# Two feature blocks of a gated feed-forward product by seven half-block products

## The chip, the cores and the metric

The kernel runs on one core of a Trainium2 chip. The metric is the device time of one execution in microseconds (us); smaller is better. The core's engines, as the profile names them: PE is TensorE (matmuls; PEld its weight loads), DVE is VectorE, ACT is ScalarE, POOL is GpSimd, SP is SyncE, which here only issues DMAs. All engines run their own instructions in program order and wait for each other by semaphores. SBUF is the memory that all engines work in, PSUM the one that TensorE writes its results to; PSUM is used here in eight banks of 512 f32 values for each of 128 partitions.

## The reference

Attention with projected keys and values (8 batches, 8 heads, 1024 positions, head size 64, 64 projected keys), whose output is the input of a gated feed-forward layer (8192 tokens, model width 512, hidden width 1536):

```python
k_proj = einsum('ks,bhsd->bhkd', E, k)
v_proj = einsum('ks,bhsd->bhkd', F, v)
scores = (q @ k_proj^T) / sqrt(64)
x = softmax(scores) @ v_proj            # then heads side by side: 8192 x 512
g = x @ w_gate
silu = g / (1 + exp(-g))
val = x @ w_val
out = (silu * val) @ w_out
```

The inputs are f32; the kernel loads them as bf16 and multiplies in bf16 with f32 sums.

## The kernel before

The 8192 tokens are worked in 16 chunks of 512 (c = 0 to 15), two for each batch: chunk 2b and chunk 2b + 1. For each chunk, `xT` holds the attention output transposed: 128 partitions x 4 blocks of the model width x 512 tokens. The hidden width is worked in 12 blocks of 128 features (f = 0 to 11). The main loop at the end of the program runs over all (c, f), with counter t = 12c + f; each turn has two slots, 2t and 2t + 1, into which the next batch's attention work is put by hand.

One turn:

- `f_g(c, f)`: the gate product, four matmuls of 512 tokens into a bank `gps` (pool "g", two banks), then ScalarE's SiLU into an f32 tile `th` (line 541). In some blocks, listed in `TANGENT`, a tanh and two VectorE operations (lines 538, 553, 556) take its place; blocks 10 and 11 of chunks 2 to 14 are not among them.
- slot 2t
- `f_v(c, f)`: the value product, four matmuls of 512 into a bank `vps` (pool "v", two banks in turn), then VectorE multiplies `th` by it into `hT[c][:, f]` (line 550)
- what `late[t]` holds: the output product of the chunk before, and sums for it
- slot 2t + 1

The output product (`f_m`, lines 676 to 686) already goes by seven products of half blocks (Strassen). For each of two token halves p it makes products m = 3, 4, 5, 2, 1, 6, 7, each of six matmuls of 256 columns (line 634), at blocks 0, 1, 2, 3, 4, 4, 5 for p = 0 and 6, 7, 8, 9, 10, 10, 11 for p = 1 of the chunk that follows. Products 3, 4, 5, 2 share a bank "y", and 1, 6, 7 a bank "z". Between them come `m_34` (ScalarE copy, GpSimd sum L653), `m_52` (ScalarE copy L658), `m_16` (VectorE L663, GpSimd L664) and `m_7` (VectorE L669, and the output DMA on SP's queue). The sums of hidden blocks that these products need are `h_sum` (line 617): m = 5 and 2 on GpSimd, one feature pair (f, f + 6) at a time as soon as block f + 6 is done (blocks 6 to 11); m = 1, 6, 7 on VectorE, whole, in blocks 1 to 3 of the next chunk.

Attention for the next batch in the slots: `u_KV` (projections, L176, evacuated by ScalarE L184 and VectorE L189), `u_S` (scores L367 and exponential L375), `u_R` (row sum L397 and reciprocal L398 on VectorE), `u_N` (division L412 and a running check L428 on GpSimd), `u_AD` and `u_TD` (transposes by DMA on SP's queue), and `u_PVt` (L471), which makes `xT` with four ScalarE copies (L480) out of the banks "a", "a", "y", "z". `u_PVt` stands in block 10 of chunk 2 and of the odd chunks 3 to 13, and in block 4 of the even chunks 4 to 14. `u_R` for the next batch falls into blocks 7 and 9 of the even chunks 4 to 12, and into blocks 8 and 10 of chunk 2.

Loads of q, k and v for the next batch are issued from GpSimd's queue. q has a pool of four buffers, `s1` one of three.

Of the kernel before, what the change touches and what calls it, by code (L numbers as in the profile page):

```python
# [9 lines left out]
AF = mybir.ActivationFunctionType  # L10
ALU = mybir.AluOpType
AX = mybir.AxisListType
BF16 = mybir.dt.bfloat16
FP32 = mybir.dt.float32

B = 8
H = 8
S = 1024
D = 64
# [3 lines left out]
P = 128  # L23
# [3 lines left out]
NFT = DFF // P  # L27
CH = 2
CW = 512
NIT = B * CH * NFT  # L30
NC = B * CH
HF = NFT // 2
HC = DM // 2
HT = CW // 2
ENG = [getattr(mybir.EngineType, n) for n in ("PE", "DVE", "Activation", "SP", "Pool")]
TANGENT = [(c, f) for c in range(CH) for f in range(NFT)] + [
    x for b in range(2, B) for x in ((2 * b - 2, 8 if b == 2 else 7), (2 * b - 1, 1))
]
BY_DMA = [(b, ch) for b in range(1, B) for ch in range(CH)]


@with_exitstack
def kernel(
# [19 lines left out]
    nc = tc.nc  # L63
# [2 lines left out]
    const = ctx.enter_context(tc.tile_pool(name="const", bufs=1))  # L66
    w_pool = ctx.enter_context(tc.tile_pool(name="weights", bufs=1))
    kv_pool = ctx.enter_context(tc.tile_pool(name="kv", bufs=1))
    q_pool = ctx.enter_context(tc.tile_pool(name="qbf", bufs=4))
    aw = ctx.enter_context(tc.tile_pool(name="aw", bufs=2))  # L70
    x_pool = ctx.enter_context(tc.tile_pool(name="xT", bufs=1))
    h_pool = ctx.enter_context(tc.tile_pool(name="hT", bufs=2))
    fw = ctx.enter_context(tc.tile_pool(name="fw", bufs=3))
# [22 lines left out]
    wv = w_pool.tile([P, NKT, DFF], BF16, name="wv")  # L96
# [3 lines left out]
    kb, vb, qb, xT, hT = {}, {}, {}, {}, {}  # L100
# [3 lines left out]
    def batch(t, b):  # L104
        return t[bass.ds(turn_of[0], 1)].rearrange("o h s d -> (o h) s d") if turn_of else t[b]

    def load_k(b, h0=0, h1=H):
        if b or maxed:
            kb[b] = kv_pool.tile([P, H, NJ, D], BF16, name="kb", tag="kb")
        nc.gpsimd.dma_start(  # L110
            out=kb[b][:, h0:h1].rearrange("p h j d -> p h (j d)"),
            in_=batch(k, b)[h0:h1].rearrange("h (p j) d -> p h (j d)", j=NJ),
        )
# [10 lines left out]

    def load_q(b, ch, js=(0, 4), hs=(0, H)):
        if js[0] == 0 and hs[0] == 0:
            qb[b, ch] = q_pool.tile([P, H, 4, D], BF16, name="qb", tag="qb")
        js, hs = slice(*js), slice(*hs)
        nc.gpsimd.dma_start(  # L129
            out=qb[b, ch][:, hs, js, :].rearrange("p h j d -> p h (j d)"),  # L130
            in_=batch(q, b)[hs].rearrange("h (p c j) d -> p c h j d", c=2, j=4)[:, ch, :, js, :].rearrange(
                "p h j d -> p h (j d)"
            ),
        )
# [16 lines left out]
    maxed = []  # L151
# [4 lines left out]
    def bank(where, shape, dt, name):  # L156
        if where == "a" and ring["wide"]:
            where = "aaz"[ring["n"] % 3]
            ring["n"] += 1
        pool, tag = banks[where]  # L160
        return pool.tile(shape, dt, name=name, tag=tag)
# [150 lines left out]
    qT, ee, rr, AA, AT = {}, {}, {}, {}, {}  # L312
    by_dma = list(BY_DMA)

# [195 lines left out]
    gp = {}  # L510
# [3 lines left out]
    def f_mm(c, f, w, i=None):  # L514

        if i != 1:


            where = "y" if (c, f, w) == (0, 2, 0) else "gv"[w]
            half[c, f, w] = bank(where, [P, CW], FP32, where + "ps")  # L520
        ps = half[c, f, w]
        x = xT[divmod(c, CH)]
        ts = slice(0, CW) if i is None else slice(256 * i, 256 * (i + 1))
        for kt in range(NKT):
            nc.tensor.matmul(  # L525
                out=ps[:, ts],
                lhsT=(wg, wv)[w][:, kt, f * P : (f + 1) * P],
                rhs=x[:, kt, ts],
                start=(kt == 0),
                stop=(kt == NKT - 1),  # L530
            )
        return ps

    def f_g(c, f, i=None):
        ps = f_mm(c, f, 0, i)
        th = fw.tile([P, CW], FP32, name="th", tag="th")
        if (c, f) in TANGENT and not maxed:
            nc.scalar.activation(out=th[:], in_=ps[:], func=AF.Tanh, scale=0.5)  # L538
            gp[0] = (ps, th)
        else:  # L540
            nc.scalar.activation(out=th[:], in_=ps[:], func=AF.Silu)  # L541
            gp[0] = (None, th)

    def f_v(c, f, i=None):
        ps = f_mm(c, f, 1, i)
        g, th = gp.pop(0)
        if f == 0:
            hT[c] = h_pool.tile([P, NFT, CW], BF16, name="hT", tag="hT")
        if g is None:
            nc.vector.tensor_tensor(out=hT[c][:, f, :], in0=th[:], in1=ps[:], op=ALU.mult)  # L550
            return
        s1 = fw.tile([P, CW], FP32, name="s1", tag="s1")
        nc.vector.scalar_tensor_tensor(
            out=s1[:], in0=th[:], scalar=1.0, in1=g[:], op0=ALU.add, op1=ALU.mult
        )
        nc.vector.scalar_tensor_tensor(
            out=hT[c][:, f, :], in0=s1[:], scalar=0.5, in1=ps[:], op0=ALU.mult, op1=ALU.mult
        )
# [226 lines left out]
    def general():  # L785
# [6 lines left out]
        with tc.For_i(0, B) as turn, tc.manual_schedule():  # L792
            turn_of.append(turn)
            b = 0
            load_k(b)
            load_v(b)
            u_KV(b)
            u_KT(b)
            for ch in range(CH):
                c = CH * b + ch  # L800
                load_q(b, ch)
                for u in range(4 * ch, 4 * ch + 4):
                    u_T(b, u)
                    u_S(b, u)
                    u_R(b, u)
                    u_N(b, u)
                    u_A(b, u)
                u_PVt(b, ch, (0, 1), ("aa", "yz"))
                for f in range(NFT):
                    f_g(c, f)  # L810
                    f_v(c, f)
                for m in (1, 2, 5, 6, 7):
                    h_sum(c, m, 0, HF, nc.vector)
                for n in range(14):
                    f_m(c, n)

    with tc.manual_schedule():
# [3 lines left out]
        for i in range(2):  # L821
            nc.scalar.dma_start(
                out=kraw[i][:],
                in_=k[0, 2 * i : 2 * i + 2].rearrange("h (p j) d -> p h (j d)", j=NJ),
# [4 lines left out]
        ]  # L829
        nc.sync.dma_start(out=ef[0][:], in_=E)  # L830
        load_q(0, 0, (0, 2))
        load_k(0, 4, 8)
        zeros = fw.tile([P, CW], BF16, name="zeros", tag="s1")
        nc.vector.memset(zeros[:], 0.0)
        make_identity(nc, ident_fp[:])
        make_identity(nc, ident_bf[:])
# [24 lines left out]

        dve, act = nc.vector, nc.scalar
        load_q(0, 0, (2, 4))
        nc.gpsimd.dma_start(out=ef[1][:], in_=F)
        load_v(0, (0, 4, 6, 8))
# [5 lines left out]
        for h in range(4):  # L871
            for n in range(2):
                eng = act if (h, n) == (3, 1) else dve
# [90 lines left out]
        late = defaultdict(list)  # L964
# [4 lines left out]
        for c in range(1, NC):  # L969
            for f in range(HF):  # L970
                for m in (5, 2):
                    late[c * NFT + HF + f].append((h_sum, c, m, f, f + 1))
            if c == NC - 1:
                late[c * NFT + HF].append((h_sum, c, 6, 0, HF, nc.vector))
                for f in (0, 2, 4):
                    for m in (1, 7):
                        late[c * NFT + HF + f + 1].append((h_sum, c, m, f, f + 2, nc.vector))
            else:
                for i, m in enumerate((1, 6, 7)):
                    late[(c + 1) * NFT + 1 + i].append((h_sum, c, m, 0, HF, nc.vector))  # L980
                for n, f in enumerate((0, 1, 2, 3, 4, 4, 5, 6, 7, 8, 9, 10, 10, 11)):
                    late[(c + 1) * NFT + f].append((f_m, c, n))

        for s, fn in ((38, u_sum), (40, u_flag), (88, u_bad)):
            put(48 * (B - 2) + s, fn)
        for t in range(NIT):
            c, f = divmod(t, NFT)
            ring["wide"] = c < 2
            i = 1 if t < 2 else None
            f_g(c, f, i)  # L990
            run_slot(2 * t)
            f_v(c, f, i)
            for fn, *a in late.pop(t, ()):
                fn(*a)
            run_slot(2 * t + 1)
# [34 lines left out]
```

## Time and profile before

| what | us |
|---|---|
| median of 3 runs (548.88 to 549.53) | 549.27 |
| the profiled execution: its time | 548.71 |
| the profiled execution: span from first to last instruction | 547.2 |
| TensorE matmuls busy | 534.7 |
| VectorE busy | 317.3 |
| GpSimd busy | 303.7 |
| ScalarE busy | 262.2 |
| one 512-wide operation on VectorE, L550: mean | 0.684 |
| one 256-wide operation on VectorE, L663: mean | 0.422 |
| h_sum on GpSimd, 128x256 bf16: mean (shortest 0.657, longest 1.321) | 0.686 |
| h_sum on VectorE, 128x1536 bf16: mean (most often 0.95, longest 1.462) | 1.089 |

The granted TensorE clock of the core is 0.998 of full speed. A chunk in the steady part takes some 32.5 us, a block 2.38 us, or 3.0 us where two output products stand in it.

How to read it: busy time is the union of an engine's instructions. A matmul's row gives its latency (0.273 us for 256 columns), while the next one starts 0.109 us after it; so the pitch is read from the start times of rows that follow each other, not from the mean. In a timeline, equal instructions of one engine are merged ("x4") and the second number is from the first start to the last end. "[0.62 <-PE yps L634]" means that the engine was idle for 0.62 us before, until that instruction ended.

### The profile page before, as it was taken

The numbers are of one execution on the slowest core, as the hardware profiler recorded it, in microseconds if no ns is written. First come the engines' busy times: TensorE is split into PE (matmuls) and PEld (weight loads), VectorE is DVE, ScalarE is ACT, GpSimd is POOL, SyncE is SP. The second block draws the span as 40 slices with busy tenths as digits, with TensorE's granted clock in tenths as the row PEclk, the third lists the DMA queues.
The fourth block names the chain that finished last, engine by engine and source line by source line (L and its number), as shares of the span: only waits on it lengthen the run. The fifth ranks groups of instructions, "written<-read, shape, count | busy, mean of one in ns | idle before, by whom it ended". The sixth has DMA issues, their size and how long they took to land.

```text
span 547.2 us, 9325 instructions
## 1 busy us (share of the span) xinstructions
PE 534.7 (98%) x3496; PEld 314.1 (57%) x3558; DVE 317.3 (58%) x546; ACT 262.2 (48%) x441; POOL 303.7 (56%) x428
## 2 busy tenths in 40 slices
PE   8999999999999999999999999999999999999996
PEld 4654545555556655556555565566555665555665
DVE  3787895557347654667456483465735765343553
ACT  3564454574446634556435554455444663443331
POOL 6962494487616864096632966258661666416172
PEclk9999999999999999999999999999999999999999
DMA  9999969929931797109930199114990123011003
GB/s 201 192 196 191 167 145 185 178 77 147 205 73 40 145 208 149 40 2 200 208 94 38 56 185 218 45 40 94 206 201 2 39 78 78 38 40 40 13 27 120
DMA packets 112226, 62.92 MB, mean 115 GB/s; under 512 B 65968, under 2 KB 103856, under 8 KB 112176
## 3 DMA queue, kind: packets, MB, share of 16 engines
q0 software_dynamic: 43952, 29.49, 37.6%
q1 hardware_dynamic: 67392, 31.46, 24.3%
q10 hardware_dynamic: 832, 1.31, 0.8%
q8 instruction: 29, 0.48, 0.3%
q14 instruction: 21, 0.17, 0.1%
HBM read 60.29 MB, written 16.78 MB: 141 GB/s over the span
## 4 chain that ended last, share of the span: by engine, by line
PE 94%; DMA 2%; POOL 1%; issue 1%; ACT 0%; DVE 0%; POOLq 0%; DVEq 0%; ACTq 0%
PE vps L525 30%; PE gps L525 29%; PE yps L634 25%; PE sc L367 3%; DMA wv<-in_moe_w_val_dram 2%; PE kvp L176 2%; PE yps L568 2%; PE pv L471 1%; POOL vb L120 0%; POOL qb L129 0%; POOL AA L412 0%; PE kvp L215 0%; PE kvp L200 0%; PE qTp L332 0%; PE pv L451 0%
## 5 line engine op out<-in xcount | busy, mean ns | idle before, releaser
L525 PE MATMUL vps<-xT,wv 128*128 128x512 bf16 (+1 forms) x755 | 195.4, 377 | 2.0 <-DMA wv<-in_moe_w_val_dram 0.9
L525 PE MATMUL gps<-xT,wg 128*128 128x512 bf16 (+1 forms) x733 | 193.0, 377 | 1.7
L550 DVE TENSOR_TENSOR hT<-th,vps 128x512 bf16<-128x512 f32 x156 | 106.7, 684 | 146.7 <-PE vps L525 121.5
L541 ACT ACTIVATE th<-gps 128x512 f32<-128x512 f32 x156 | 93.2, 597 | 176.1 <-PE gps L525 156.0
L617 POOL TENSOR_TENSOR hs<-hT 128x256 bf16<-128x256 bf16 x180 | 118.6, 686 | 40.6 <-DVE hT L550 40.0
L525 PEld LDWEIGHTS <-wv 128*128 128x128 bf16 x776 | 74.1, 98 | 91.0 <-issue 6.5
L634 PEld LDWEIGHTS <-hs 128*128 128x128 bf16 x900 | 88.1, 98 | 34.6 <-issue 0.6
L525 PEld LDWEIGHTS <-wg 128*128 128x128 bf16 x776 | 74.1, 98 | 51.4 <-issue 0.2
L664 POOL TENSOR_TENSOR tt<-tt,ysb 128x512 f32<-128x512 f32 x28 | 35.5, 1269 | 101.5 <-DVE tt L663 101.5
L412 POOL TENSOR_TENSOR AAd<-ee,zr 128x512 bf16<-128x512 f32 x56 | 58.4, 1043 | 41.6 <-ACT ee L375 17.6
L634 PE MATMUL yps<-ws,hs 128*128 128x256 bf16 x540 | 68.6, 273 | 0.2 <-DVE ysb L703 0.2
L397 DVE TENSOR_REDUCE zr<-ee 128x8 f32<-128x512 f32 x64 | 43.4, 678 | 20.4 <-ACT ee L375 20.4
L617 DVE TENSOR_TENSOR hs<-hT 128x1536 bf16<-128x1536 bf16 (+1 forms) x49 | 50.0, 1026 | 0.1
L634 PE MATMUL yps<-ws,hT 128*128 128x256 bf16 x360 | 48.8, 273 | 0.3
L634 PE MATMUL yps<-wo,hs 128*128 128x256 bf16 x360 | 48.6, 273 | 0.1
L653 POOL TENSOR_TENSOR tt<-xs 128x256 f32<-128x256 f32 x30 | 22.9, 763 | 39.7 <-ACT xs L651 39.7
L634 PEld LDWEIGHTS <-hT 128*128 128x128 bf16 x360 | 35.2, 98 | 16.0
L375 ACT ACTIVATE ee<-sc 128x512 f32<-128x512 f32 x64 | 35.7, 606 | 4.3 <-PE sc L367 2.9
L658 ACT COPY ysb<-yps 128x512 f32<-128x512 f32 x30 | 17.6, 586 | 27.3 <-PE yps L634 27.3
L651 ACT COPY xs<-yps 128x512 f32<-128x512 f32 x30 | 17.7, 590 | 25.1 <-PE yps L634 25.0
L538 ACT ACTIVATE th<-gps 128x512 f32<-128x512 f32 x35 | 20.9, 598 | 16.5 <-PE gps L525 16.5
L480 ACT CAST xT<-pv 128x512 bf16<-128x512 f32 x56 | 28.8, 599 | 0.0
(112 smaller groups left out, 403.7 us busy)
## 6 DMA issues: line engine op xcount, KB each, us to landing
out_dram<-ysb SPq DMA_DIRECT2D x27, 512.0 KB, 3.0
qb<-in_q_dram POOLq DMA_DIRECT2D x14, 512.0 KB, 15.2
kb<-in_k_dram POOLq DMA_DIRECT2D x7, 1024.0 KB, 10.0
vb<-in_v_dram POOLq DMA_DIRECT2D x7, 1024.0 KB, 14.8
wo<-in_moe_w_out_dram POOLq DMA_DIRECT2D x2, 768.0 KB, 21.6
out_dram<-ysb SPq DMA_DIRECT2D x6, 256.0 KB, 2.4
kraw<-in_k_dram ACTq DMA_DIRECT2D x2, 512.0 KB, 4.7
qb<-in_q_dram POOLq DMA_DIRECT2D x4, 256.0 KB, 7.9
```

The source lines that it names most:

```text
L375: nc.scalar.activation(out=e[:].rearrange("p h j k -> p (h j k)"), in_=ps[:].rearrange("p a k -> p (a k)"), func=AF.Exp, scale=scale,)
L397: nc.vector.reduce_sum(out=z, in_=e[:], axis=AX.X)
L412: eng.tensor_tensor(out=a.rearrange("p j h k -> p h j k"), in0=ee.pop((b, u))[:], in1=r.unsqueeze(3).to_broadcast([P, 4, 2, KP]), op=ALU.mult,
L480: nc.scalar.copy(out=xT[b, ch][:, kt, :], in_=ps[:])
L525: nc.tensor.matmul(out=ps[:, ts], lhsT=(wg, wv)[w][:, kt, f * P : (f + 1) * P], rhs=x[:, kt, ts], start=(kt == 0), stop=(kt == NKT - 1),)
L538: nc.scalar.activation(out=th[:], in_=ps[:], func=AF.Tanh, scale=0.5)
L541: nc.scalar.activation(out=th[:], in_=ps[:], func=AF.Silu)
L550: nc.vector.tensor_tensor(out=hT[c][:, f, :], in0=th[:], in1=ps[:], op=ALU.mult)
L617: eng.tensor_tensor(out=hs[c, m][:, fs, :], in0=quarter(hT[c], *a)[:, fs], in1=quarter(hT[c], *b)[:, fs], op=op,)
L634: nc.tensor.matmul(out=ps, lhsT=lhsT, rhs=ws[m][:, f, :] if rhs is None else rhs, start=(start and f == 0), stop=(f == HF - 1), skip_group ...
L653: nc.gpsimd.tensor_tensor(out=t[:, 0], in0=xs[:, 0], in1=xs[:, 1], op=ALU.add)
L664: nc.gpsimd.tensor_tensor(out=t[:], in0=t[:], in1=yo[c, p][:, 1:3], op=ALU.subtract)
```

## The change

In chunks 2 to 14 the value products of blocks 10 and 11 are made together. They are a product of a 256 x 512 weight by a 512 x 512 input; both are cut into two by two halves (weights: 128 features x 256 model; input: 256 model x 256 tokens), and the four result quarters come from seven products of halves in place of eight, each of two matmuls of 256 tokens. The sums of weight halves are made once, in chunk 2, on VectorE (`p_w`); the sums of input halves for every chunk (`p_x`), on GpSimd in even chunks (blocks 2, 3, 3, 5) and on VectorE in odd ones (blocks 6 to 9). SiLU of blocks 10 and 11 goes into one tile `thp`. The value product of block 10 makes products 3, 4 and 1, that of block 11 products 5, 2, 6 and 7, with seven VectorE operations that put the quarters together and multiply.

For the space, q's pool goes from four to two buffers and the two of batch 0 get tags of their own, whose space the sums use later; `s1` goes from three buffers to one. The `h_sum` of m = 5 and 2 for the last two feature pairs moves from blocks 10 and 11 behind block 0 of the next chunk.

```diff
+PAIR = (10, 11)
+PAIRED = range(2, NC - 1)
...
-    q_pool = ctx.enter_context(tc.tile_pool(name="qbf", bufs=4))
+    q_pool = ctx.enter_context(tc.tile_pool(name="qbf", bufs=2))
...
-            qb[b, ch] = q_pool.tile([P, H, 4, D], BF16, name="qb", tag="qb")
+            if b or maxed:
+                qb[b, ch] = q_pool.tile([P, H, 4, D], BF16, name="qb", tag="qb")
+            else:
+                qb[b, ch] = q_pool.tile([P, H, 4, D], BF16, name="qb", tag=f"q0{ch}", bufs=1)
...
     def f_g(c, f, i=None):
         ps = f_mm(c, f, 0, i)
+        if paired(c, f):
+            if f == PAIR[0]:
+                gp["p"] = fw.tile([P, 2, CW], FP32, name="thp", tag="thp", bufs=1)
+            nc.scalar.activation(out=gp["p"][:, f - PAIR[0]], in_=ps[:], func=AF.Silu)
+            return
...
+    def p_x(c, m, eng):
...
+        i0, i1, op = {
+            67: (x[:, :, 0:HT], x[:, :, HT:CW], ALU.add),
+            1: (b[0, 0], b[1, 1], ALU.add),
+            3: (b[0, 1], b[1, 1], ALU.subtract),
+            4: (b[1, 0], b[0, 0], ALU.subtract),
+        }[m]
+        eng.tensor_tensor(out=sums["x", m], in0=i0, in1=i1, op=op)
...
+    def p_mm(c, m, ps, start=False):
...
+        for kt in range(2):
+            nc.tensor.matmul(
+                out=ps,
+                lhsT=w[:, kt],
+                rhs=xs[:, kt],
+                start=(start and kt == 0),
+                stop=(kt == 1),
+                skip_group_check=True,
+            )
+
+    def f_v_pair(c, f):
+
+        tensor_tensor = nc.vector.tensor_tensor
+        if f == PAIR[0]:
+            xp = gp["x"] = bank("v", [P, 2, HT], FP32, "vps")
+            t = gp["t"] = fw.tile([P, 2, HT], FP32, name="vt", tag="s1", bufs=1)
+            p_mm(c, 3, xp[:, 0], start=True)
+            nc.vector.tensor_copy(out=t[:, 0], in_=xp[:, 0])
+            p_mm(c, 4, xp[:, 1])
+            tensor_tensor(out=t[:, 0], in0=t[:, 0], in1=xp[:, 1], op=ALU.add)
+            zp = gp["z"] = bank("v", [P, 2, HT], FP32, "vps")
+            p_mm(c, 1, zp[:, 0], start=True)
+            tensor_tensor(out=t[:, 1], in0=t[:, 0], in1=zp[:, 0], op=ALU.add)
+            return
+        th, xp, zp, t = (gp.pop(i) for i in "pxzt")
+        th = th[:].rearrange("p i t -> p (i t)")
+        h = hT[c][:, PAIR[0] : PAIR[1] + 1, :].rearrange("p i t -> p (i t)")
+        p_mm(c, 5, xp[:, 0])
+        p_mm(c, 2, xp[:, 1])
+        tensor_tensor(out=t[:], in0=t[:], in1=xp[:], op=ALU.subtract)
+        tensor_tensor(
+            out=h[:, HT : 3 * HT], in0=th[:, HT : 3 * HT], in1=xp[:].rearrange("p i t -> p (i t)"), op=ALU.mult
+        )
+        p_mm(c, 6, zp[:, 1])
+        p_mm(c, 7, zp[:, 0])
+        tensor_tensor(out=t[:], in0=t[:], in1=zp[:], op=ALU.add)
+        h, th = (a.rearrange("p (i t) -> p i t", i=4)[:, 0::3] for a in (h, th))
+        tensor_tensor(out=h, in0=th, in1=t[:], op=ALU.mult)
+
     def f_v(c, f, i=None):
+        if paired(c, f):
+            return f_v_pair(c, f)
...
-        s1 = fw.tile([P, CW], FP32, name="s1", tag="s1")
+        s1 = fw.tile([P, CW], FP32, name="s1", tag="s1", bufs=1)
...
-                    late[c * NFT + HF + f].append((h_sum, c, m, f, f + 1))
+                    late[c * NFT + (NFT if paired(c, HF + f) else HF + f)].append((h_sum, c, m, f, f + 1))
...
+        for f, m in ((3, 1), (3, 2), (3, 5), (4, 6), (4, 7)):
+            late[2 * NFT + f].append((p_w, m))
+        for c in PAIRED:
+            for i, m in enumerate((67, 1, 3, 4)):
+                f, eng = ((2, 3, 3, 5)[i], nc.gpsimd) if c % 2 == 0 else (6 + i, nc.vector)
+                late[c * NFT + f].append((p_x, c, m, eng))
```

More of the change, by code (lines that the diff above doesn't have):

```diff
@@ L532, in f_mm, with paired @@
         return ps
+    def paired(c, f):
+        return f in PAIR and c in PAIRED and not maxed
     def f_g(c, f, i=None):
         ps = f_mm(c, f, 0, i)
+        if paired(c, f):
[3 more added lines that the diff above has]
+            return
         th = fw.tile([P, CW], FP32, name="th", tag="th")
@@ L542, in f_g, with p_tiles @@
             gp[0] = (None, th)
+    sums = {}
+    def p_tiles():
+        a = q_pool.tile([P, 8, HT], BF16, name="xsa", tag="q00", bufs=1)
+        b = q_pool.tile([P, 14, P], BF16, name="xsb", tag="q01", bufs=1)
+        x4 = b[:, 0:4].rearrange("p (k n) t -> p k (n t)", k=2)
+        for m, x in ((6, a[:, 0:2]), (7, a[:, 2:4]), (67, a[:, 0:4]), (1, a[:, 4:6]), (3, a[:, 6:8]), (4, x4)):
+            sums["x", m] = x
+        for i, m in enumerate((1, 2, 5, 6, 7)):
+            sums["w", m] = b[:, 4 + 2 * i : 6 + 2 * i]
@@ new lines, in p_w @@
+    def p_w(m):
+        f = [slice(i * P, (i + 1) * P) for i in PAIR]
+        a = {(i, j): wv[:, 2 * j : 2 * j + 2, f[i]] for i in range(2) for j in range(2)}
+        x, y, op = {
+            1: ((0, 0), (1, 1), ALU.add),
+            2: ((1, 0), (1, 1), ALU.add),
+            5: ((0, 0), (0, 1), ALU.add),
+            6: ((1, 0), (0, 0), ALU.subtract),
+            7: ((0, 1), (1, 1), ALU.subtract),
+        }[m]
+        nc.vector.tensor_tensor(out=sums["w", m], in0=a[x], in1=a[y], op=op)
@@ new lines, in p_x @@
+    def p_x(c, m, eng):
+        if not sums:
+            p_tiles()
+        x = xT[divmod(c, CH)]
+        b = {(i, j): x[:, 2 * i : 2 * i + 2, HT * j : HT * (j + 1)] for i in range(2) for j in range(2)}
+        i0, i1, op = {
[3 more added lines that the diff above has]
+            4: (b[1, 0], b[0, 0], ALU.subtract),
+        }[m]
+        eng.tensor_tensor(out=sums["x", m], in0=i0, in1=i1, op=op)
@@ new lines, in p_mm @@
+    def p_mm(c, m, ps, start=False):
+        x = xT[divmod(c, CH)]
+        f = [slice(i * P, (i + 1) * P) for i in PAIR]
+        w = {3: wv[:, 0:2, f[0]], 4: wv[:, 2:4, f[1]]}[m] if m in (3, 4) else sums["w", m]
+        xs = {2: x[:, 0:2, 0:HT], 5: x[:, 2:4, HT:CW]}[m] if m in (2, 5) else sums["x", m]
+        for kt in range(2):
[7 more added lines that the diff above has]
+            )
@@ L832 @@
         load_k(0, 4, 8)
-        zeros = fw.tile([P, CW], BF16, name="zeros", tag="s1")
+        zeros = fw.tile([P, CW], BF16, name="zeros", tag="thp", bufs=1)
         nc.vector.memset(zeros[:], 0.0)
```

## The prediction

> **What bounds the kernel now.** I read the page first: busy times, granted clock, the chain that ended last.
>
> ```profile
> PE 534.7 (98%) x3496; PEld 314.1 (57%) x3558; DVE 317.3 (58%) x546; ACT 262.2 (48%) x441; POOL 303.7 (56%) x428
> ...
> PEclk9999999999999999999999999999999999999999
> ...
> PE 94%; DMA 2%; POOL 1%; issue 1%; ACT 0%; DVE 0%; POOLq 0%; DVEq 0%; ACTq 0%
> ```
>
> TensorE is busy for 98% of the span at full clock and is 94% of the chain, so a matmul saved is time saved, and a wait put into TensorE's stream is time lost one for one: there is no slack to take it up. The other engines are busy for about half of the span; what they get costs nothing until TensorE waits for it.
>
> Next the timeline of steady chunks, where the change acts: in block 10 of an even chunk (10) and of the odd one after it (11).
>
> ```profile
> 370.46 0.68 DVE L397 TENSOR_REDUCE zr<-ee 128x8 f32<-128x512 f32 x1
> ...
> 370.75 1.03 PE L525 MATMUL vps<-xT,wv 128*128 128x512 bf16 x4
> ...
> 371.17 0.20 DVE L398 RECIPROCAL zr<-zr 128x8 f32<-128x8 f32 x1
> ...
> 371.62 1.47 PE L634 MATMUL yps<-ws,hs 128*128 128x256 bf16 x12
> ...
> 372.93 1.03 PE L525 MATMUL gps<-xT,wg 128*128 128x512 bf16 x4
> ```
>
> ```profile
> 402.19 1.04 PE L525 MATMUL vps<-xT,wv 128*128 128x512 bf16 x3
> 402.31 2.05 ACT L480 CAST xT<-pv 128x512 bf16<-128x512 f32 x4
> ...
> 403.06 1.47 PE L634 MATMUL yps<-ws,hs 128*128 128x256 bf16 x12
> ...
> 404.64 0.42 DVE L663 TENSOR_TENSOR tt<-tt,yps 128x256 f32<-128x256 f32 x1 [0.62 <-PE yps L634]
> ```
>
> Columns: start, length, engine, line, operands. The reader takes three things from them. Pitches: four 512-wide matmuls take 371.62 - 370.75 = 0.86 (0.2159 each from the exact starts), twelve 256-wide ones 372.93 - 371.62 = 1.31 (0.1092 each), with other weights each time. In even chunks VectorE is busy with a row sum until 371.37, 0.62 into the value product; in odd ones it is idle there. And the row of L663: it reads the left half of a bank, product m=1, the first six of the twelve matmuls (their end 403.06 + 5 x 0.109 + 0.273 = 403.88), yet it starts 0.11 after the end of all twelve (404.53), though the other six fill the right half only. VectorE was idle for 0.62 before it.
>
> The same from another place, in the list of waits and the timeline of chunk 10:
>
> ```profile
> DVE VS L189 <- ACT ks L184: 17.5, 6, 3.0
> ```
>
> ```profile
> 354.88 0.59 ACT L184 CAST ks<-kvp 64x512 bf16<-64x512 f32 x1
> ...
> 355.51 0.87 DVE L189 CAST VS<-kvp 64x256 bf16<-64x256 f32 x2 [3.00 <-ACT ks L184]
> ```
>
> L189 reads partitions 64 to 127 of a bank, L184 partitions 0 to 63; no number passes between them. Still L189 starts 0.04 after L184 ends, six times out of six. So the semaphores of this program keep two engines apart by the whole bank, not by the bytes touched.
>
> **What is removed.** In each of 13 chunks eight 512-wide matmuls go (8 x 0.2159 = 1.727) and fourteen 256-wide ones come (14 x 0.1092 = 1.529): 0.198 saved, 2.58 in all. Per block: the value product of 10 shrinks from 0.864 to 6 x 0.1092 = 0.655, that of 11 grows to 0.874. The weight loads (98 ns each) hide under 109 as they do in the row of L634. The Trainium skill, "TensorE: Matmul & The Clock Gate", "Back-to-back issue gap", gives about 131 ns for a 512-wide matmul in a sustained stream and 81 for a 128-wide one; by that eight would cost 1.05 and fourteen at least 1.13, no saving at all. The measured 215.9 decides: the page's isolated formula fits this stream, its sustained figure doesn't.
>
> **What is added on TensorE's path.** In block 10 the code issues product 3 into the left half of bank xp, then a VectorE copy of that half, then product 4 into the right half of the same bank. If banks are guarded whole, product 4 waits for the copy, and product 1 and everything else of TensorE queue behind it; those who wait for TensorE (SiLU of block 11, m_16) come later with it. Let T be the start of the value product. Product 3's second matmul starts at T + 0.109 and ends 0.273 later: 0.382. One wait more: 0.04 (SiLU starts 0.03 after its matmuls; L663 with two waits 0.11). Copy begins T + 0.42. The copy, 256 f32 elements out of PSUM, isn't in the trace; nearest rows:
>
> ```profile
> L164 DVE CAST xT<-pv 128x256 bf16<-128x256 f32 x2 | 0.8, 418 | 1.4 <-PE pv L500 1.4
> L164 DVE COPY FT<-efp 128x256 bf16<-128x256 bf16 x1 | 0.3, 291 | 0.4 <-PE efp L844 0.4
> L663 DVE TENSOR_TENSOR tt<-tt,yps 128x256 f32<-128x256 f32 x28 | 11.8, 422 | 13.2 <-PE yps L634 12.9
> ```
>
> I take 0.42 (same source type and size); bounds 0.29 and 0.42. Back to TensorE: 0.05 (in the tail an L703 of 0.415 from 540.32 on lets TensorE go on at 540.79). So product 4 starts at T + 0.89 in place of T + 0.218: 0.67 lost. That holds for the chunks where VectorE is idle at T + 0.42: 3, 5, 7, 9, 11, 13, 14 (no scores follow in 14). In 4, 6, 8, 10, 12 the row sum and reciprocal hold it until T + 0.62 (371.37 above), so the copy starts at T + 0.65: 0.90. In chunk 2 they end at T + 0.68: 0.97. Sum 7 x 0.67 + 5 x 0.90 + 0.97 = 10.2. Bounds: with the 0.29 copy 13 x 0.13 = 1.7 less; if the row sum got out of the way 6 x 0.23 = 1.4 less; with a second wait at the copy 0.07 more each, 0.9.
>
> The Trainium skill, "PSUM — Partial Sum Buffer", "PSUM bank collisions raise a hardware error", asks for just this guard: a TensorE write and a VectorE access to one bank and the same 32 partitions, even at other columns, is an error, so the order must be kept by bank. It speaks against this change: by bank the result is 556.9, by address it would be 547.4. No row of this trace shows such a collision.
>
> **What hides.** VectorE gets per chunk three 256-wide operations (0.42) and four 512-wide (0.69, as L550 and L669), less two L550 (1.37): +2.65, 34 in all; in odd chunks also the input sums, 2560 bf16 elements at L617's 0.95 per 1536, 1.6. GpSimd gets them in even chunks: 2560 at its L617's 0.67 per 256, at most 6.7, in the 9.39 that it idles before L664; beside them VectorE's L617 may go from 0.95 to the 1.46 seen when GpSimd ran, which leaves 0.69 + 1.46 within the 2.38 of a block. The five weight sums, 256 elements each, come once. In block 11 the subtraction starts at 0.64 to 0.70 of the value product (the end of product 2), the multiplication that frees xp ends two times 0.69 later, 2.07 to 2.13 with the way back; the next chunk's first value product needs that bank at 0.874 + 0.655 + 0.864 = 2.39. A cover of 0.27; if it is gone, each 0.1 more costs 1.3. The last four sums of m=5 and m=2 on GpSimd move behind the next chunk's first block: VectorE's chain 2.8, then 4 x 0.67; the product m=5 comes 7.1 to 8.0 after block 11's value product (406.10 to 413.25; 374.65 to 382.69), so 1.6 or more to spare. One key load passes them in GpSimd's queue, 0.94 to issue; it still fits. Output rows and their DMA on SP's queue come some 1.4 later, and the transposes behind them too; the attention weights that they make are used ten blocks later. q's two buffers: the transposes that free them end at 67.2 where the next load is issued at 80.2; later batches have more. In chunks 2, 3, 5 .. 13 the attention product's ScalarE copies (row L480) free a bank at 402.90, 0.05 more for TensorE; a value product of 0.655 would need it at 402.85, 0.1 lost. The copy's wait covers that.
>
> **Sum.** +10.2 - 2.6 = +7.6 on the profiled 547.2 (its run took 548.71, 1.5 around the span, unchanged). Median of the runs 549.27, so 556.9.
>
> **Rivals.** (a) Product 4 doesn't wait: a guard by half banks. For it: f_m waits for one bank's copy of the four L480, so waits are fine-grained between banks. Against it: L663 and L189 above. Then 2.58 saved less 7 x 0.1 = 0.7: 547.4, faster; it decides if product 4's matmuls follow at 0.109. 8%. (b) Guarded, and in block 11 VectorE falls behind: an output addition (L669, 0.69) or a row sum gets ahead of the multiplication, and the next chunk's value product waits for xp: (0.69 - 0.27) x 13 = 5.5 more, 562.4. For it: a cover of only 0.27. Against: in program order L669 stands behind the pair's chain, and row sums fall into block 11 in chunk 2 alone. 6%. (c) The forecast, 86%: own range 553.8 (both lower bounds) to 559.5 (second waits 0.9, and 0.13 a chunk of overrun in block 11).
>
> **Numbers.** 556.9; range 553.8 to 559.5, which leaves out (a) and (b), 14%. A measurement of this kernel tells 0.2%, 1.1, from no change: faster 0.08 from (a), within 0.02 for a wait mostly hidden, slower 0.90.
>
> **What would show it.** In block 10 a gap of 0.67 (odd) or 0.90 (even) on TensorE before product 4, ended by the copy; fourteen 256-wide matmuls at 0.109; TensorE's busy time down by about 2.6 and its idle time up by 10; no wait in the next chunk's first value product; L617 on GpSimd ending before m=5. I am wrong if product 4 follows product 3 without a gap, or if the copy takes much less than 0.42.

## The result, and the profile after

The changed kernel takes 555.38 us (median of 5 runs, 555.30 to 557.14), before 549.27 (5 runs): ratio 1.0118, 95% interval 1.0102 to 1.0133. It is slower by 6.1 us; the forecast was 7.6. The profiled executions have spans of 553.8 and 547.2 us, 6.6 apart.

The page of the changed kernel, its busy times and the chain that ended last (by engine):

```profile
PE 537.7 (97%) x3636; PEld 320.8 (58%) x3636; DVE 369.4 (67%) x640; ACT 262.0 (47%) x441; POOL 356.3 (64%) x456
...
PE 87%; ACT 4%; POOL 3%; DMA 2%; DVE 2%; issue 2%; ACTq 0%; POOLq 0%; DVEq 0%
```

VectorE has 52 us more and GpSimd 53 us more than before, and neither is near the span. TensorE is still the bound, and its share of the chain falls from 94% to 87%. That share alone proves no loss: in two of the runs below, the copy behind product 4 and the sums alone, it is 87% as well, and neither is slower than before. Its busy time rises by 3.0, where the forecast had it fall by 2.6. Two things in the page hide the fall: of before's 3558 matmuls (the count of the weight loads) 62 rows are missing, of the changed kernel's 3636 none; and a matmul ahead of a gap counts its whole latency of 0.27, not the 0.11 up to the next one, 13 times. A missing 512-wide row leaves a hole of some 0.05 (two pitches of 0.216 less a latency of 0.38), 3.3 for the 62; with 13 x 0.16 = 2.1 that is 5.4 of the 5.6 between the forecast and the page. So the saving is read from pitches.

The timeline of the changed kernel in block 10 of an odd chunk (9), where VectorE had nothing else to do:

```profile
341.08 0.39 PE L602 MATMUL vps<-xsa,wv 128*128 128x256 bf16 x2
...
341.51 0.42 DVE L618 COPY vt<-vps 128x256 f32<-128x256 f32 x1 [1.31 <-PE vps L602]
341.99 0.38 PE L602 MATMUL vps<-xsb,wv 128*128 128x256 bf16 x2 [0.52 <-DVE vt L618]
...
342.21 0.38 PE L602 MATMUL vps<-xsa,xsb 128*128 128x256 bf16 x2
```

The three rows of L602 are products 3, 4 and 1. Product 3 fills the left half of the bank; VectorE copies that half from 341.51 to 341.94; product 4, which fills the right half, starts at 341.99, 0.05 after the copy's end, and not at 341.08 + 2 x 0.109 = 341.30. Product 1 follows without a gap. The gap is 0.68.

The same in the even chunk 10:

```profile
374.78 0.68 DVE L402 TENSOR_REDUCE zr<-ee 128x8 f32<-128x512 f32 x1
...
375.08 0.38 PE L602 MATMUL vps<-xsa,wv 128*128 128x256 bf16 x2
...
375.49 0.20 DVE L403 RECIPROCAL zr<-zr 128x8 f32<-128x8 f32 x1
375.61 0.37 DVE L618 COPY vt<-vps 128x256 f32<-128x256 f32 x1
375.79 0.22 POOL L433 TENSOR_TENSOR zsum<-zsum,zr 128x16 f32<-128x16 f32 x1
...
376.04 0.11 PEld L602 LDWEIGHTS <-wv 128*128 128x128 bf16 x2 [0.86 <-DVE vt L618]
376.04 0.39 PE L602 MATMUL vps<-xsb,wv 128*128 128x256 bf16 x2 [0.58 <-POOL zsum L433]
```

Here the copy waits for the row sum and the reciprocal, and the gap is 376.04 - 375.08 - 0.218 = 0.74. The label of the matmul names GpSimd's L433, which ended at 376.01; product 4 reads and writes nothing of it. It ended by chance between the copy's end, 375.98, and product 4: the profile infers a releaser. The weight load that goes with the matmul names the copy, and so do the odd chunks, where L433 isn't there.

### The profile page after: what moved, and what is told of

It reads as the page before. It is cut to its first block, busy times and chain, and to the rows that moved or that the text cites. A ratio compares the mean times of both kernels' runs of the same rounds, so it can differ in the third digit from the quotient of the medians.

```text
span 553.8 us, 9681 instructions
## 1 busy us (share of the span) xinstructions
PE 537.7 (97%) x3636; PEld 320.8 (58%) x3636; DVE 369.4 (67%) x640; ACT 262.0 (47%) x441; POOL 356.3 (64%) x456
## 4 chain that ended last, share of the span: by engine, by line
PE 87%; ACT 4%; POOL 3%; DMA 2%; DVE 2%; issue 2%; ACTq 0%; POOLq 0%; DVEq 0%
PE gps L530 27%; PE vps L530 24%; PE yps L732 23%; PE vps L602 4%; DMA wv<-in_moe_w_val_dram 2%; PE sc L372 2%; PE kvp L181 2%; PE yps L666 2%; ACT L554 1%; PE pv L476 1%; ACT ee L380 1%; POOL AAd L417 1%; DVE hT L648 1%; POOL hs L715 1%; ACT th L554 1%
## 5 line engine op out<-in xcount | busy, mean ns | idle before, releaser
L530 PE MATMUL gps<-xT,wg 128*128 128x512 bf16 (+1 forms) x772 | 196.6, 377 | 0.0
L530 PE MATMUL vps<-xT,wv 128*128 128x512 bf16 (+1 forms) x672 | 170.9, 377 | 0.7 <-DMA wv<-in_moe_w_val_dram 0.7
L715 POOL TENSOR_TENSOR hs<-hT 128x256 bf16<-128x256 bf16 x180 | 120.7, 695 | 53.6 <-DVE hT L648 30.6
L554 ACT ACTIVATE th<-gps 128x512 f32<-128x512 f32 x130 | 77.6, 597 | 151.3 <-PE gps L530 142.1
L648 DVE TENSOR_TENSOR hT<-th,vps 128x512 bf16<-128x512 f32 x130 | 88.6, 681 | 80.4 <-PE vps L530 66.5
L530 PEld LDWEIGHTS <-wv 128*128 128x128 bf16 x672 | 64.4, 98 | 77.6 <-issue 3.8
L732 PEld LDWEIGHTS <-hs 128*128 128x128 bf16 x900 | 88.0, 98 | 29.1 <-issue 0.6
L732 PE MATMUL yps<-ws,hs 128*128 128x256 bf16 x540 | 68.6, 273 | 0.2 <-DVE ysb L801 0.2
L715 DVE TENSOR_TENSOR hs<-hT 128x1536 bf16<-128x1536 bf16 (+1 forms) x49 | 60.1, 1231 | 0.1
L732 PE MATMUL yps<-ws,hT 128*128 128x256 bf16 x360 | 48.8, 273 | 0.0
L732 PE MATMUL yps<-wo,hs 128*128 128x256 bf16 x360 | 48.6, 273 | 0.1
L732 PEld LDWEIGHTS <-hT 128*128 128x128 bf16 x360 | 35.2, 98 | 16.1
L593 POOL TENSOR_TENSOR xsa<-xT 128x512 bf16<-128x512 bf16 (+1 forms) x21 | 40.4, 1950 | 0.0
L547 ACT ACTIVATE thp<-gps 128x512 f32<-128x512 f32 x26 | 15.5, 598 | 31.7 <-PE gps L530 31.7
```

Source lines behind the costliest of these rows:

```text
L530: nc.tensor.matmul(out=ps[:, ts], lhsT=(wg, wv)[w][:, kt, f * P : (f + 1) * P], rhs=x[:, kt, ts], start=(kt == 0), stop=(kt == NKT - 1),)
L593: eng.tensor_tensor(out=sums["x", m], in0=i0, in1=i1, op=op)
L715: eng.tensor_tensor(out=hs[c, m][:, fs, :], in0=quarter(hT[c], *a)[:, fs], in1=quarter(hT[c], *b)[:, fs], op=op,)
L732: nc.tensor.matmul(out=ps, lhsT=lhsT, rhs=ws[m][:, f, :] if rhs is None else rhs, start=(start and f == 0), stop=(f == HF - 1), skip_group ...
```

## The experiments

The starts of all matmuls of L602 give the gap ahead of product 4 in each of the 13 chunks: 0.80 in chunk 2, 0.68 in the seven chunks 3, 5, 7, 9, 11, 13, 14, and 0.75 in 4, 6, 8, 10, 12; 9.29 in all. With the 2.58 saved that is +6.7, the measured 6.6 of the spans. That is a sum that fits; the experiments take the gap away, shrink it, lengthen it, and put the rest of the change alone. Their runs stand beside runs of the kernel before on the same chip: 549.09 (16 runs) for the first four, 549.01 for the last.

**The copy behind product 4.**

```diff
-            nc.vector.tensor_copy(out=t[:, 0], in_=xp[:, 0])
             p_mm(c, 4, xp[:, 1])
+            nc.vector.tensor_copy(out=t[:, 0], in_=xp[:, 0])
```

> The copy of product 3 stands behind product 4, nothing else is changed. Theory (the loss is the wait of product 4 for the copy, because the whole bank is guarded): the 13 gaps in block 10 (9.3 us in the trace of the changed kernel) are gone, the 2.6 us of the two matmuls saved per chunk stay, and in the seven blocks with the attention product in it the output product waits some 0.1 us for ScalarE's copy of its bank: 549.27 - 2.58 + 0.7 = 547.4. Rival 1 (part of the loss is the load of VectorE and GpSimd or their contention): above 549.3. Rival 2 (the wait moves: the copy now starts at 0.64 of the value product, and VectorE is late in block 11): gaps before product 5 or before the next chunk's first value product, and 549 or more.

Measured: 546.81 (6 runs), ratio 0.9963 (0.9951 to 0.9976), faster than before. Two lines in another order are worth 8.6 us against the change as it was. The time is 0.6 under the expected one; the six runs lie between 546.40 and 548.32. The timeline of this kernel in block 10 of chunk 9:

```profile
336.11 0.39 PE L602 MATMUL vps<-xsa,wv 128*128 128x256 bf16 x2
336.23 2.05 ACT L485 CAST xT<-pv 128x512 bf16<-128x512 f32 x4
336.34 0.38 PE L602 MATMUL vps<-xsb,wv 128*128 128x256 bf16 x2
...
336.56 0.38 PE L602 MATMUL vps<-xsa,xsb 128*128 128x256 bf16 x2
...
336.76 0.42 DVE L619 COPY vt<-vps 128x256 f32<-128x256 f32 x1 [1.52 <-PE vps L602]
336.87 1.47 PE L732 MATMUL yps<-ws,hs 128*128 128x256 bf16 x12
```

Products 3, 4, 1 follow each other, the copy comes after them, and no gap appears at product 5 or at the next chunk's first value product: the two additions that now end later are needed only in block 11. The copy shows the guard from its other side: it reads product 3 alone, which ended at 336.50, and VectorE was idle, yet it starts at 336.76, 0.04 after the end of product 4 in the other half of the bank. The output product (L732) starts 336.87 - 336.56 = 0.31 after product 1's first matmul in place of 0.22: the 0.09 that it waits for ScalarE's first copy (L485), in each of the seven chunks that have it, 0.60 in all by the exact starts, against the 0.7 expected.

**Product 6 in block 10 too.** The edit stands on top of the one before.

```diff
             p_mm(c, 1, zp[:, 0], start=True)
+            p_mm(c, 6, zp[:, 1])
...
-        p_mm(c, 6, zp[:, 1])
         p_mm(c, 7, zp[:, 0])
```

> As e1_copy_after_4, and product 6 moves from block 11 to block 10 (eight half matmuls in block 10, six in block 11). Theory: the value product of block 10 takes 0.874 again, so the output product no longer comes before ScalarE's copy, and the seven waits of 0.1 us go: 546.7, 0.7 under e1_copy_after_4. Bound: block 11 is shorter by 0.218, so the bank xp is needed at 2.17 of it, and VectorE frees it at about 1.98; no wait there. Rival: there was no wait of 0.1 us in e1_copy_after_4 (equal times), or the bank xp comes too late (0.1 us each, 1.3 us in all, slower than e1_copy_after_4).

Measured: 545.94 (5 runs), ratio 0.9944 (0.9930 to 0.9957): the best version, 3.2 faster than before and 9.4 faster than the change as it was. In its timeline of chunk 9 the output product follows at the pitch of 0.109:

```profile
336.14 2.05 ACT L485 CAST xT<-pv 128x512 bf16<-128x512 f32 x4
...
336.47 0.60 PE L602 MATMUL vps<-xsa,xsb 128*128 128x256 bf16 x4
...
336.90 1.47 PE L732 MATMUL yps<-ws,hs 128*128 128x256 bf16 x12
```

336.90 - 336.47 = 0.43 for four matmuls. No gap is left at either block in any of the 13 chunks, and the bank xp came free in time. The step from the first variant is 0.87 by the medians, 0.60 by the gaps; the intervals of the two ratios overlap by 0.0006, so the gaps that are gone carry this reading, not the times alone.

**The sums alone.**

```diff
     def f_g(c, f, i=None):
         ps = f_mm(c, f, 0, i)
-        if paired(c, f):
+        if False:
...
     def f_v(c, f, i=None):
-        if paired(c, f):
-            return f_v_pair(c, f)
```

> The value products of blocks 10 and 11 are made as in the kernel before (eight matmuls of 512, one multiplication each); the input and weight sums on VectorE and GpSimd are still made, though nothing reads them, the last h_sums stand behind the next chunk's first block, and the buffers are those of the changed kernel. Theory (all of this is hidden): 549.3, within 0.5. Rival 1 (load and contention cost): 550.5 to 555, with TensorE waiting for VectorE or for an h_sum.

Measured: 548.94 (10 runs), ratio 0.9998 (0.9989 to 1.0008): no difference. Its page:

```profile
PE 535.4 (98%) x3496; PEld 313.8 (57%) x3558; DVE 339.4 (62%) x575; ACT 262.2 (48%) x441; POOL 355.7 (65%) x456
```

Of what the change adds, 52 of GpSimd's 53 us and 22 of VectorE's 52 are there, at no cost. The rival in which load or contention pays for a part falls. The other 30 us of VectorE, the seven operations of the pair less the two multiplications that they replace, are in the first two variants, which are faster than before.

**Product 1 between the copy and product 4.**

```diff
+            zp = gp["z"] = bank("v", [P, 2, HT], FP32, "vps")
             p_mm(c, 3, xp[:, 0], start=True)
             nc.vector.tensor_copy(out=t[:, 0], in_=xp[:, 0])
+            p_mm(c, 1, zp[:, 0], start=True)
             p_mm(c, 4, xp[:, 1])
             tensor_tensor(out=t[:, 0], in0=t[:, 0], in1=xp[:, 1], op=ALU.add)
-            zp = gp["z"] = bank("v", [P, 2, HT], FP32, "vps")
-            p_mm(c, 1, zp[:, 0], start=True)
```

> The changed kernel with product 1 (in the other bank) put between the copy and product 4, so that the copy has 0.218 us of TensorE work over it. Theory: each of the 13 gaps shrinks by 0.218, from 9.29 to 6.46 in all: 549.27 - 2.58 + 6.46 = 553.1. If the gap were a price of the pair that doesn't depend on the copy (rival 3: a switch between value banks, or issue): unchanged, 555.4.

Measured: 552.64 (4 runs), ratio 1.0065 (1.0049 to 1.0080). Chunk 9:

```profile
339.62 0.39 PE L602 MATMUL vps<-xsa,wv 128*128 128x256 bf16 x2
...
339.85 0.38 PE L602 MATMUL vps<-xsa,xsb 128*128 128x256 bf16 x2
...
340.05 0.42 DVE L619 COPY vt<-vps 128x256 f32<-128x256 f32 x1 [1.31 <-PE vps L602]
340.53 0.38 PE L602 MATMUL vps<-xsb,wv 128*128 128x256 bf16 x2 [0.29 <-DVE vt L619]
```

Product 1 goes to the other bank and runs at once, while VectorE waits for product 3 and then copies it; product 4 again starts 0.05 after the copy. The gaps sum to 6.44 against 6.46 expected. So it is the bank that is being read, not the pair as such, that holds TensorE, and what stands in between counts in full.

**The copy twice.**

```diff
             nc.vector.tensor_copy(out=t[:, 0], in_=xp[:, 0])
+            nc.vector.tensor_copy(out=t[:, 0], in_=xp[:, 0])
```

> The changed kernel with VectorE's copy of product 3 made twice, the same bytes both times. Theory (product 4 waits until VectorE is done with the bank): each of the 13 gaps grows by one more copy, 0.37 (behind another instruction) to 0.42, so 4.8 to 5.5 in all: 555.4 + 5.1 = 560.5. Rival 3 (the gap is a price that doesn't go with the copy's length): 555.4.

Measured: 561.42 (4 runs), ratio 1.0225 (1.0208 to 1.0242). The price of one more copy was set too low: the gaps grow by 0.46 each, to 15.24 in all, 5.95 more, which is the 6.0 between the medians. The two copies in chunk 9:

```profile
344.56 0.42 DVE L618 COPY vt<-vps 128x256 f32<-128x256 f32 x1 [1.31 <-PE vps L602]
345.02 0.42 DVE L619 COPY vt<-vps 128x256 f32<-128x256 f32 x1
345.50 0.38 PE L602 MATMUL vps<-xsb,wv 128*128 128x256 bf16 x2 [0.97 <-DVE vt L619]
```

They start 0.46 apart: the second, which writes the same bytes, begins 0.04 after the first has ended, and doesn't overlap with it as the copy in the even chunks overlaps with the reciprocal. The rival in which the gap doesn't go with the copy's length falls.

## Why the prediction was right

**The mechanism** was right in each step: product 4 waits for the copy of the other half of its bank, product 1 queues behind it, the wait is paid one for one, and nothing else is. Taking the copy out of the way leaves the saving, and rival (a), a guard by half banks, is refuted by every one of the 13 gaps. Whether the guard goes by the bank or by the tile wasn't separated: a tile here is a bank.

**The saving**: 0.198 a chunk, 2.58 in all, was forecast. The pitch of the fourteen 256-wide matmuls is 0.109 in the changed kernel, and the best variant is 2.7 under the kernel before by the spans and 3.2 by the medians. The sustained figure of about 131 ns for a 512-wide matmul, by which nothing would be saved (the Trainium skill, "TensorE: Matmul & The Clock Gate", "Back-to-back issue gap"), doesn't hold here: in the steady part of the changed kernel too these matmuls follow each other at 0.216.

**The wait** was mis-sized, 10.2 against 9.29. In the chunks with an idle VectorE 0.67 was forecast and 0.68 measured, step by step: copy at 0.43 after the start of product 3 (forecast 0.42), 0.425 long (0.42), 0.05 back (0.05). In the even chunks 0.90 was forecast and 0.75 measured, in chunk 2 0.97 and 0.80. The step that failed is "hold it until T + 0.62, so the copy starts at T + 0.65": the copy started at T + 0.53, before the reciprocal's row ended, and took 0.37 in place of 0.42. It needs nothing of the reciprocal, and its row overlaps the reciprocal's by 0.08 in all six of these chunks. The rows before showed such overlaps: in the timeline of chunk 10, L398 starts at 371.17, 0.03 behind the end of L397, whose sums it needs, while L397 itself starts at 370.46, before the end (370.54) of an L550 that has nothing for it:

```profile
369.89 0.65 DVE L550 TENSOR_TENSOR hT<-th,vps 128x512 bf16<-128x512 f32 x1
```

In that trace the dependent pair, L397 and L398, is 0.03 apart 64 times of 64, and an L550 that follows an L398 overlaps it by 0.08 in 11 of 11. Not every independent pair overlaps (of two 64-partition casts, L288 starts 0.01 after L287). So adding a row's full length to a queue put the copy 0.12 too late.

**The base** accounts for the rest. The sum was made for the profiled execution, 547.2 + 7.6 = 554.8, and measured 553.8: 1.0 too high, of which the wait is 0.9. The profiled run before, 548.71, was 0.56 under its median, and that of the changed kernel is its median; carried to the median of before, the same sum reads 1.5 too high.

**What hides** was right: no gap before product 5 or the next chunk's first value product, so rival (b) fell. Its cover was 0.27 by the forecast; in chunk 10 the multiplication ends at 380.59 and the bank is taken at 381.05, which with 0.05 for the way back leaves 0.41, and it is the same in every chunk. The last h_sums end at 384.54 and product m=5 starts at 387.57: 3.0 to spare there and in the other even chunks up to 12, and 2.1 in the odd ones and 14, where at least 1.6 was forecast. Chunk 10 and the start of the next:

```profile
379.91 0.68 DVE L631 TENSOR_TENSOR hT<-thp,vps 128x512 bf16<-128x512 f32 x1
...
381.05 1.03 PE L530 MATMUL vps<-xT,wv 128*128 128x512 bf16 x4
...
382.00 2.54 POOL L715 TENSOR_TENSOR hs<-hT 128x256 bf16<-128x256 bf16 x4 [1.22 <-DVE hT L638]
...
387.57 0.82 PE L732 MATMUL yps<-wo,hs 128*128 128x256 bf16 x6
```

The wait of 0.1 for ScalarE's copy is not seen in the changed kernel, being covered by the gap, and comes out at 0.09 as soon as the gap is gone.

**What was wrong without a price**: that TensorE's busy time would show the saving (it falls in the first variant, 532.4 against 534.7, where both traces lack 62 rows), and the lengths of the input sums, on GpSimd "at most 6.7" where 2.1 + 2 x 1.87 + 1.16 = 7.0 was measured, on VectorE 1.6 where 0.90 + 2 x 0.46 + 0.42 = 2.24 was.

## What to carry to other kernels

When results of half a bank are interleaved, put every write of a bank before the first read of it, or let something in another bank stand between: a write, a read and a write cost one round trip of 0.68 here, 3.4 times what the algebra saved in a chunk. Read from the trace before what the semaphores guard, by finding a reader that waits longer than its data needs. And when work is removed from the bound engine, look for the next thing that it then reaches too early, since the 0.09 behind ScalarE's copy was hidden in the slow version and worth 0.6 us in the fast one.

## What the runs showed of the hardware that was not expected

Sums of bf16 on VectorE and GpSimd take longer side by side, and by more than the trace before had shown. The costliest groups of the changed kernel, same shapes apart (count, busy us, mean ns of one):

```profile
L715 DVE TENSOR_TENSOR hs<-hT 128x1536 bf16<-128x1536 bf16 x43 | 56.9, 1323 | 0.0
...
L593 POOL TENSOR_TENSOR xsa<-xT 128x512 bf16<-128x512 bf16 x14 | 25.9, 1867 | 0.0
...
L593 POOL TENSOR_TENSOR xsa<-xT 128x1024 bf16<-128x1024 bf16 x7 | 14.8, 2116 | 0.0
...
L593 POOL TENSOR_TENSOR xsb<-xT 128x512 bf16<-128x512 bf16 x7 | 8.1, 1157 | 0.0
```

VectorE's h_sum went from a mean of 1.089 to 1.323, and one of 128x1536 that took 0.95 in block 2 of chunk 10 took 2.05 when GpSimd made its sum of 128x1024 beside it, as in block 2 of all seven even chunks:

```profile
353.49 2.05 DVE L715 TENSOR_TENSOR hs<-hT 128x1536 bf16<-128x1536 bf16 x1
355.47 0.67 DVE L648 TENSOR_TENSOR hT<-th,vps 128x512 bf16<-128x512 f32 x1
```

On GpSimd 512 elements take 1.16 in block 5, where no h_sum runs on VectorE, and 1.87 in block 3. TensorE didn't notice, but 0.69 + 2.05 is over the 2.38 of a block: the forecast had allowed for 1.46, and it held because the next block's multiplication was only 0.2 late (355.47, where 352.89 + 2.38 = 355.27 was its turn). The cause of the stretch was not tried by itself.
